# Fewer, larger transfers on one queue: weight copies of three rows, and one store for each output block

## The chip, the core and the metric

The kernel runs on one core of a Trainium2 chip. The metric is the time of one execution on the device in microseconds (us), and the median over runs is compared. TensorE is called PE below, VectorE DVE, ScalarE ACT, GpSimd POOL and SyncE SP, as in the profile. SP computes nothing: its instructions issue DMA transfers, in order, on one hardware queue.

## The reference

Attention with a sigmoid in place of the softmax, followed by a token-mixing layer that makes its mixing weights from its own input. All inputs and the output are float32.

```python
# q, k, v: (8, 12, 448, 64)
scores = q @ k^T / sqrt(64) - log(448)          # per batch and head
attn   = sigmoid(scores) @ v
x      = attn, heads side by side               # (8, 448, 768)
wq, wk = x @ w_q, x @ w_k                       # w_q, w_k: (768, 64)
W      = wq wk^T / sqrt(64)                     # (448, 448) per batch, token to token
mixed  = W @ x                                  # computed as wq @ (wk^T @ x)
out    = relu(mixed) @ w_out                    # w_out: (768, 768)
```

## The kernel before

**Units of work.** The 12 heads of a batch are taken in groups of four, a *quad*; there are 8 x 3 = 24 of them. For a quad, q, k and v are loaded (each 448.0 KB of float32 on 128 partitions), cast to bfloat16 mostly by POOL, arranged and transposed, and then seven score tiles are formed by PE (L319), put through the sigmoid by ACT (L324), and multiplied with v by PE (L341). The 448 tokens are dealt out as 64 partitions of 7 tokens each. When the three quads of a batch are done, the token-mixing layer follows for that batch.

**The order of work** is a string of letters written out by hand, `PLAN`, which is walked once while the program is built: `S` a score tile, `P` a values tile, `C` a copy of output weights, `O` (and `o`, `Q`, `I`, `i`) a part of the output product, and so on. Each engine executes what falls to it in that order and waits on semaphores for what it needs. Where a letter issues a DMA, it goes to SP at that place. The loads have an order of their own, `ORDER`; a load is issued as soon as one of the eight load buffers is free, which is when the load eight places before it has been cast. SP waits for that buffer in its queue, and what was put behind the load waits too.

**The output weights** lie in `wout16`, an array of 128 partitions x 12 rows x 768 columns in bfloat16. Rows 0 to 5 are w_out as loaded, by two transfers of POOL. Rows 6 to 11 are the second arrangement: the same six rows with the two halves of the partitions exchanged. It is made by DMA copies inside the on-chip memory (L864), two for each letter `C`, one row each. Only the batches 2 to 5 use it: their output products (`out_pair`, L530) work on quarters of the PE array, take a half of the contraction from each half of the partitions, and step through the row numbers given by `slot`; twelve steps in four groups of three, of which the last two groups use rows 9 to 11 of the arrangement.

**The output** of a pair of batches `w` is formed in blocks. For the pairs 0 and 3 a block `m` is 128 rows: two tokens per partition group, `y` = 0 in partitions 0 to 63 and `y` = 1 in partitions 64 to 127, with 768 columns. The product (L611) is formed in two halves of 384 columns, each copied from PSUM into the array `o` by ACT or DVE (L644), and then `store` (L621) sends the array out: one transfer for each `y`, 64 partitions x 768 columns. Token `i` of batch `b` goes to rows `i`, `7 + i`, `14 + i`, ... of that batch's output. Block `m` = 3 of a pair has its first half in one batch and its second in the next. Some blocks are formed by another function (`out_halves`, L570, stores at L584), and the pairs 1 and 2 by `out_pair` (copied at L541 or L543, stored at L551). All three take `o` from one pool of three arrays, so the fourth block after another writes into the array from which that one was stored, once that store has landed.

After the last score tile the kernel is in its *tail*: `store` then uses SP for one half and ACT's queue for the other. The last block of all is stored in pieces of 384 columns or fewer.

Of the kernel before, what the change touches and what calls it, by code (L numbers as in the profile page):

```python
# [17 lines left out]
def kernel(  # L18
# [12 lines left out]
    nc = tc.nc  # L31
    B, H, S, HD = q.shape
    D = H * HD
# [3 lines left out]
    NI, NP = 7, 64  # L37
    NU = B
    NJ = H // 4
    NC = D // P  # L40
    NB = D // 2
    HALF = (slice(0, 64), slice(64, 128))
# [45 lines left out]
    def bank2():  # L88
        lo, hi = (int(b) for b in BANKS.pop())
        take(lo, hi)  # L90
        assert hi == lo + 1
        return (lo, hi), banks[:, lo : hi + 1], banks16[:, lo : hi + 1]

    def bank1():
        b = int(BANKS.pop())
        take(b)
        return (b,), banks[:, b], banks16[:, b]

    def read(fb, inst, keep=False):

        for b in fb:
            for old in readers[b][0]:
                if not keep and old.ins.engine != inst.ins.engine:
                    tc.declare_no_dep(inst.ins, old.ins, reason="both only read the bank")
            readers[b][1].append(inst)

    wout16 = singles.tile([P, 2 * NC, D], BF16, name="wout16")
# [406 lines left out]
    def slot(half, b):  # L514

        return b // 2 + (0 if b % 2 == half else NC)

    def out_pair(act, split):

        if opened:  # L520
            w, blocks, part, fb, ps = opened.pop()
        else:
            w, blocks = chunks.pop(0)
            part = 0
            fb, ps, _ = bank2()
        mx = mxs[w].rearrange("p (u b x) -> p u b x", u=2, b=12)
        for b in range(3 * part, 3 * part + 3):
            for y, (u, i) in enumerate(blocks):
                for x in range(2):
                    nc.tensor.matmul(  # L530
                        ps[HALF[x], y, 0:NB], mx[HALF[y], u, b, 64 * (i - 3 * y) : 64 * (i - 3 * y) + 64],
                        wout16[HALF[y], slot(y, b), x * NB : (x + 1) * NB],
                        start=(b == 0), stop=(b == 11),
                    )
        if part < 3:
            opened.append((w, blocks, part + 1, fb, ps))
            return
        o = p_o.tile([P, 2, NB], F32, tag="o", name="o")
        if split:
            for y in range(2):  # L540
                read(fb, COPY["vs"[y]](out=o[:, y], in_=ps[:, y, 0:NB]), keep=True)  # L541
        else:
            read(fb, COPY["s" if act else "v"](out=o, in_=ps[:, :, 0:NB]), keep=True)  # L543
        (u0, i0), (u1, i1) = blocks
        for x in range(2):
            cols = slice(x * NB, (x + 1) * NB)
            if u0 == u1:
                dst = out[2 * w + u0].rearrange("(p i) d -> p i d", i=NI)[:, i0 : i1 + 1 : i1 - i0, cols]
            else:
                dst = out[2 * w : 2 * w + 2].rearrange("b (p i) d -> i p b d", i=NI)[i0, :, :, cols]  # L550
            nc.sync.dma_start(out=dst, in_=o[HALF[x]])  # L551
# [41 lines left out]
    def out_chunk(act, tail):  # L593

        if opened:
            w, m, nb, fb, ps = opened.pop()
            part = 1
        else:
            w, m, nb = chunks.pop(0)
            if nb < 0:  # L600
                nb = 0
                chunks.insert(0, (w, m, 1))
            fb, ps, _ = bank1()
            part = 0
        if nb == 0 and not part:
            ot[0] = p_o.tile([P, D], F32, tag="o", name="o")
        o = ot[0]

        def block(ps, w0, w1, c0, c1):
            for c in range(c0, c1):  # L610
                nc.tensor.matmul(  # L611
                    ps, mxs[w][:, 2 * S * c + m * P : 2 * S * c + (m + 1) * P],
                    wout16[:, c, w0:w1], start=(c == 0), stop=(c == NC - 1),
                )

        last = w == NU // 2 - 1 and m == NI - 1

        def store(cols, eng=nc.scalar if tail else nc.sync):
            for y in range(2):
                b, i = divmod(2 * m + y, NI)  # L620
                (eng if y else nc.sync).dma_start(  # L621
                    out=out[2 * w + b].rearrange("(p i) d -> p i d", i=NI)[:, i, cols],
                    in_=o[HALF[y], cols],
                )

        if nb and last:

            if part:
                fb, ps, _ = bank1()
            h = NB // 2  # L630
            c0 = NB + part * h
            block(ps[:, 0:h], c0, c0 + h, 0, NC)
            read(fb, nc.vector.tensor_copy(out=o[:, c0 : c0 + h], in_=ps[:, 0:h]), keep=True)
            if part:
                store(slice(NB, D))
            else:
                opened.append((w, m, nb, fb, ps))
            return
        ps = ps[:, 0:NB] if not part else ps
        block(ps, nb * NB, (nb + 1) * NB, part * NC // 2, (part + 1) * NC // 2)  # L640
        if not part:
            opened.append((w, m, nb, fb, ps))
            return
        read(fb, COPY["s" if act or last else "v"](out=o[:, nb * NB : (nb + 1) * NB], in_=ps), keep=True)  # L644
        if last:
            store(slice(0, NB))
        elif nb:
            store(slice(0, D))
# [24 lines left out]
    def cols(r):  # L673
# [9 lines left out]
        out=ident, in_=ident, compare_op=ALU.not_equal, fill=1.0, base=0,  # L683
# [135 lines left out]
    for t in PLAN:  # L819
        if t == "F":  # L820
            nc.tensor.matmul(bank1()[1], zeros[:, 0:P], zeros, start=True, stop=True)
            continue
        if t in "12":
            cast_next("vs"[int(t) - 1])
            continue
        kind = ALIKE.get(t, t if t in "qkx" else t.upper())
        c = done[kind]
        done[kind] += 1
        tail = done["S"] == N * NI
        if t == "S":  # L830
            scores(*divmod(c, NI))
        elif kind == "P":
            n, i = divmod(c, NI)
            values(n, i, tail or t == "R", "s" if t == "p" else "v")
            if i == NI - 1:
                used.add(("v", n))
                pump()
        elif kind in "qk":
            if t in "rs":
                quads_r.append(c) if t == "r" else None  # L840
                if t == "s":
                    quadrants(c, 0)
            tr(c, kind, t)
            if t in "df":
                used.add(("q", c))
            if t not in "cers":
                used.add((kind, c))
                pump()
        elif t == "g":
            move()  # L850
        elif t == "z":
            n = quads_r.pop(0)
            quadrants(n, 1)
            used.update({("q", n), ("k", n)})
            pump()
        elif t == "K":
            tr_part("k", k016, KB, "v")
        elif kind == "x":
            tr_x(c, tail, t in "XY", "s" if t in "yY" else "v")
        elif kind == "W":  # L860
            mlp_wqk(*divmod(c, NC), tail, t in "wl", t in "Ll")
        elif kind == "C":
            for y in range(2):
                nc.sync.dma_start(out=wout16[HALF[y], NC + c, :], in_=wout16[HALF[1 - y], c, :])  # L864
        elif kind == "N":
            mlp_wkn(c)
        elif kind == "U":
            (mlp_tmp_tiled if t in "Tt" else mlp_tmp)(c, t in "ut")
        elif kind == "M":
            u, x = divmod(c, NC // 2)  # L870
            mlp_mix(u, x, t == "m", tail or t == "G")
            if x == NC // 2 - 1:
                if u // 2 in TW:
                    chunks.extend((u // 2, ((u % 2, i), (u % 2, 6 - i))) for i in range(3))
                    if u % 2:
                        chunks.append((u // 2, ((0, 3), (1, 3))))
                else:
                    chunks.extend((u // 2, m, -1) for m in (range(3, NI) if u % 2 else range(3)))
        elif kind == "O":
            if (opened or chunks)[0][0] in TW:  # L880
                out_pair(t == "o", t == "Q")
            elif t in "Ii":
                out_halves(t == "i")
            else:
                out_chunk(t in "oQ", tail)
            if not opened:
                allowed[0] = 2
                pump_loads()
                pump()
# [29 lines left out]
```

## Time and profile before

| | |
|---|---|
| median of 3 runs | 182.45 us |
| all three | 180.83, 182.45, 184.24 us |
| profiled execution, first to last instruction (its span) | 180.4 us |
| instructions | 7849 |
| moved by DMA | 47.29 MB, 262 GB/s over the span |
| mean granted TensorE clock | 1.000 |

The three runs are times of whole executions. Of the profiled one the profile gives the span, which is 0.4 us below the fastest run and 2.0 below the median. In the profile, L with a number is a line of the kernel; a tile is named as output `<-` inputs. A digit in a row of slices is the busy share in tenths, and a slice is a fortieth of the span, 4.5 us. Rows of DMA issues give the size of one transfer in KB of 1,024 bytes and the median time from its issue to its landing. In a row with `|`, the time before it is busy time, and behind it stands the idle time before those instructions, with what ended it.

### The profile page before, as it was taken

How to read it: one execution, taken by the hardware profiler on the slowest of the kernel's cores; microseconds unless marked ns; L12 is line 12 of the kernel's file. 1: busy time of each engine (PE TensorE's matmuls, PEld its weight loads, DVE VectorE, ACT ScalarE, POOL GpSimd, SP SyncE). 2: the span in 40 equal slices, each digit the busy share in tenths (PEclk: the TensorE clock that was granted, in tenths of full speed). 3: DMA queues.
4: the chain of work that ended last, by engine and by line, in shares of the span. 5: the costliest groups of instructions: out<-in, count | busy, mean ns of one | idle time of the engine just before them, and what ended most of it. 6: DMA issues, size and time to landing. Idle time of an engine off the chain costs nothing.

```text
span 180.4 us, 7849 instructions
## 1 busy us (share of the span) xinstructions
PE 170.3 (94%) x3412; PEld 114.1 (63%) x3412; DVE 143.7 (80%) x226; ACT 159.0 (88%) x208; POOL 122.9 (68%) x167
## 2 busy tenths in 40 slices
PE   7898899889999999999999999999999999999990
PEld 7444445444675555546667786677888888888660
DVE  3566899998988896989999999978789885868351
ACT  4599999999999999999999999998999989976310
POOL 1076899798999999999999999889978810010000
PEclk9999999999999999999999999999999999999999
DMA  5999999999999989699997999968596432505876
GB/s 169 353 394 346 325 385 376 283 304 366 339 305 358 349 266 299 226 318 349 279 318 277 257 307 329 372 215 272 137 336 166 131 88 48 137 4 123 207 196 174
DMA packets 24914, 47.29 MB, mean 262 GB/s; under 512 B 3888, under 2 KB 18480, under 8 KB 24880
## 3 DMA queue, kind: packets, MB, share of 16 engines
q1 hardware_dynamic: 23600, 44.64, 76.8%
q0 software_dynamic: 800, 1.18, 3.6%
q10 hardware_dynamic: 480, 0.98, 1.5%
q8 instruction: 26, 0.43, 0.9%
q14 instruction: 8, 0.07, 0.1%
HBM read 35.78 MB, written 11.01 MB: 259 GB/s over the span
## 4 chain that ended last, share of the span: by engine, by line
PE 61%; DMA 16%; ACT 7%; POOL 5%; DVE 4%; SPq 3%; issue 2%; POOLq 0%
PE banks L530 15%; PE banks L341 11%; PE banks L319 11%; PE banks L611 9%; DMA k<-in_k_dram 8%; ACT at L324 7%; DMA v<-in_v_dram 5%; DMA w<-in_moe_w_k_dram 4%; PE banks L570 3%; POOL qk L192 2%; PE banks L404 2%; PE banks L416 2%; PE banks L379 2%; PE banks L363 2%; PE banks L484 1%
## 5 line engine op out<-in xcount | busy, mean ns | idle before, releaser
L324 ACT ACTIVATE at<-banks 128x896 bf16<-128x896 f32 x168 | 139.8, 951 | 2.9 <-PE banks L319 2.4
L319 PE MATMUL banks<-qk 64*64 64x448 bf16 x672 | 62.0, 357 | 3.3 <-ACT at L324 2.0
L341 PE MATMUL banks<-at,v 64*64 64x448 bf16 x672 | 47.3, 351 | 0.8 <-ACT at L324 0.7
L319 PEld LDWEIGHTS <-qk 64*64 64x64 bf16 x672 | 25.7, 105 | 21.5 <-issue 13.3
L530 PE MATMUL banks<-wout,mx 64*64 64x384 bf16 x672 | 36.2, 323 | 0.0
L192 POOL CAST qk<-k 128x896 bf16<-128x896 f32 x19 | 22.7, 1196 | 10.1 <-DMA k<-in_k_dram 9.7
L341 PEld LDWEIGHTS <-v 64*64 64x64 bf16 x672 | 23.2, 106 | 8.4 <-issue 1.8
L350 DVE CAST xt<-banks 128x896 bf16<-128x896 f32 x22 | 23.8, 1084 | 2.5 <-PE banks L341 2.0
L530 PEld LDWEIGHTS <-mx 64*64 64x64 bf16 x672 | 22.6, 107 | 4.5 <-issue 0.2
L611 PE MATMUL banks<-wout,mx 128*128 128x384 bf16 (+1 forms) x138 | 24.4, 320 | 0.0
L192 POOL CAST qk<-q 128x896 bf16<-128x896 f32 x18 | 21.5, 1193 | 2.5 <-DVE qk L276 1.0
L471 DVE TENSOR_SCALAR mx<-banks 128x1024 bf16<-128x1024 f32 (+3 forms) x22 | 21.3, 970 | 1.9 <-PE banks L484 0.7
L209 POOL CAST v<-v 128x896 bf16<-128x896 f32 x22 | 20.6, 952 | 1.8 <-DMA v<-in_v_dram 1.3
L611 PEld LDWEIGHTS <-mx 128*128 128x128 bf16 x138 | 12.3, 98 | 9.8 <-issue 3.2
L167 POOL COPY qk<-swap 32x448 uint32<-32x448 uint32 x28 | 16.3, 584 | 1.6
L276 DVE STREAM_TRANSPOSE qk<-qk 128x448 f32<-128x448 f32 x28 | 17.0, 628 | 0.5 <-POOL qk L164 0.4
L161 POOL COPY swap<-qk 32x448 uint32<-32x448 uint32 x28 | 15.6, 556 | 2.5 <-DVE qk L192 0.8
L164 POOL COPY qk<-qk 32x448 uint32<-32x448 uint32 x28 | 15.6, 555 | 1.6
L245 DVE STREAM_TRANSPOSE qk<-qk 32x448 f32<-32x448 f32 x24 | 15.3, 636 | 0.6
L413 POOL COPY wq<-wqk 64x448 bf16<-64x448 bf16 x3 | 1.7, 556 | 15.8 <-DVE wqk L412 15.8
L644 DVE COPY o<-banks 128x384 f32<-128x384 f32 x12 | 6.6, 553 | 5.7 <-PE banks L611 5.3
L392 DVE COPY xn<-banks 128x1024 bf16<-128x1024 bf16 (+1 forms) x14 | 8.8, 625 | 2.8 <-PE banks L379 2.7
(89 smaller groups left out, 203.8 us busy)
## 6 DMA issues: line engine op xcount, KB each, us to landing
q<-in_q_dram SPq DMA_DIRECT2D x24, 448.0 KB, 6.3
v<-in_v_dram SPq DMA_DIRECT2D x24, 448.0 KB, 6.0
k<-in_k_dram SPq DMA_DIRECT2D x23, 448.0 KB, 6.9
out_dram<-o SPq DMA_DIRECT2D x50, 192.0 KB, 4.2
wout<-in_moe_w_out_dram POOLq DMA_DIRECT2D x2, 576.0 KB, 11.6
wout<-wout SPq DMA_DIRECT2D x12, 96.0 KB, 6.4
out_dram<-o ACTq DMA_DIRECT2D x4, 192.0 KB, 3.2
k<-in_k_dram SPq DMA_DIRECT2D x1, 256.0 KB, 4.8
```

The costliest lines, as they stand in the source:

```text
L161: eng.tensor_copy(out=z[lo], in_=w[hi, 0])
L167: eng.tensor_copy(out=w[lo, 1], in_=z[lo])
L192: COPY[e](out=f[:, :, "qk".index(nm)].rearrange("p e i d y -> p e y i d"), in_=ld.pop((nm, n)).rearrange("p (y i e d) -> p e y i d", y=2, ...
L209: COPY[e](out=t16.rearrange("p b i d -> p (b i d)"), in_=ld.pop((nm, n)).rearrange("p b x -> p (b x)"),)
L276: nc.vector.transpose(out=qk[n][:, t].rearrange("p t i n -> p (t i n)").bitcast(F32), in_=w)
L319: nc.tensor.matmul(sc[HALF[h], g, 0:S], qk[n][HALF[g], h, 1, i, :], qk[n][HALF[g], h, 0].rearrange("p i n -> p (i n)"), start=True, stop=True,
L324: inst = nc.scalar.activation(at, sc[:, :, 0:S], ACTF.Sigmoid, bias=attn_bias, scale=attn_scale)
L341: nc.tensor.matmul(ps[HALF[g], h, 0:S], ld["v16", n][HALF[h], g, i, :], ats[n, i][HALF[h], g, :], start=(i == 0), stop=(i == NI - 1),)
L350: read(fb, COPY[eng](out=xt(u, j)[:, :, 0:S], in_=ps[:, :, 0:S]))
L471: inst = nc.vector.tensor_scalar(dst, ps, moe_scale, 0.0, ALU.mult, ALU.max)
L530: nc.tensor.matmul(ps[HALF[x], y, 0:NB], mx[HALF[y], u, b, 64 * (i - 3 * y) : 64 * (i - 3 * y) + 64], wout16[HALF[y], slot(y, b), x * NB : ...
L611: nc.tensor.matmul(ps, mxs[w][:, 2 * S * c + m * P : 2 * S * c + (m + 1) * P], wout16[:, c, w0:w1], start=(c == 0), stop=(c == NC - 1),)
```

## The change

Two edits, both in what SP issues.

1. For the letter `C`, instead of two copies of one row at each of six places, one copy of three rows at four of them. Places 0 and 3 fill the first half of the partitions, places 1 and 4 the second; places 2 and 5 issue nothing.
2. Outside the tail, and where all 768 columns of a block are stored, `store` issues one transfer from the whole array `o`, 128 partitions. The destination is an access pattern written by hand, whose outermost dimension has two entries (the two tokens, `step` apart), the next 64 (steps of seven rows), and the last 768 columns.

```diff
+    def rows(b0, i0, b1, i1):
+
+        step = (b1 - b0) * S * D + (i1 - i0) * D
+        assert step > 0
+        return out[b0].rearrange("(p i) d -> p i d", i=NI)[:, i0], [step, 2]
...
         def store(cols, eng=nc.scalar if tail else nc.sync):
+            if not tail and cols == slice(0, D):
+                (b0, i0), (b1, i1) = divmod(2 * m, NI), divmod(2 * m + 1, NI)
+                at, lead = rows(2 * w + b0, i0, 2 * w + b1, i1)
+                nc.sync.dma_start(out=bass.AP(at.tensor, at.offset, [lead, [NI * D, NP], [1, D]]), in_=o)
+                return
             for y in range(2):
                 b, i = divmod(2 * m + y, NI)
                 (eng if y else nc.sync).dma_start(
...
         elif kind == "C":
-            for y in range(2):
-                nc.sync.dma_start(out=wout16[HALF[y], NC + c, :], in_=wout16[HALF[1 - y], c, :])
+            if c % 3 < 2:
+                y, lo = c % 3, c // 3 * 3
+                nc.sync.dma_start(
+                    out=wout16[HALF[y], NC + lo : NC + lo + 3, :], in_=wout16[HALF[1 - y], lo : lo + 3, :],
+                )
```

## The prediction

> **What bounds the kernel now.** I read the page first, for the span, the engines' shares and the transfers' level over time; then the chain in order of time, to see where transfers set the pace and where they don't; then the views of the SP queue, because both edits live there.
>
> ```profile
> span 180.4 us, 7849 instructions
> PE 170.3 (94%) x3412; PEld 114.1 (63%) x3412; DVE 143.7 (80%) x226; ACT 159.0 (88%) x208; POOL 122.9 (68%) x167
> DMA  5999999999999989699997999968596432505876
> GB/s 169 353 394 346 325 385 376 283 304 366 339 305 358 349 266 299 226 318 349 279 318 277 257 307 329 372 215 272 137 336 166 131 88 48 137 4 123 207 196 174
> q1 hardware_dynamic: 23600, 44.64, 76.8%
> ```
>
> The 16 DMA engines are 90% busy or close to it until about slice 26 (117 us), and nearly everything goes through one queue, q1, which is SP's. So whatever one store adds to an engine of that queue stands ahead of the loads issued after it.
>
> ```profile
> 29.29 13.64 DMA k<-in_k_dram
> ...
> 51.54 0.68 PE banks L570 x12
> ...
> 93.29 0.60 PE banks L530 x12
> ...
> 94.30 0.49 PE banks L530 x12
> ...
> 94.97 0.49 PE banks L530 x12
> ...
> 166.29 9.89 PE banks L611 x66
> 176.20 0.36 DVE o L633
> ```
>
> In the chain in order of time the last load stands at 29.29 (it lands at 42.9). From 51.5 on the chain is PE's with a few ACT pieces and no transfer. TensorE is the bound there, and a transfer counts only when it gets late enough to stop PE. PE has no spare time to win that back.
>
> Two speeds of a DMA engine are needed. The fastest slice moved 394 GB/s over 16 engines: 24.6 kB per us each. The q1 row gives the slow end: 44.64 MB in 76.8% of 16 x 180.4 us is 20.1 kB per us of busy time, waits for memory included.
>
> **The copies of the output weights.** Twelve transfers of 96 KB become four of three rows (288 KB): the bytes are the same.
>
> ```profile
> L864 SPq DMA_DIRECT2D wout<-wout x12: 467/522/897, 41.7 to 87.8; - x12
> SPq L173 <- POOL qk L192: 12.9, 7, 3.3
> SPq L179 <- POOL v L209: 8.1, 3, 4.2
> wout<-wout SPq DMA_DIRECT2D x12, 96.0 KB, 6.4
> ```
>
> Eight issues fall away, 8 x 0.52 = 4.2 us of SP. I count them as nothing: the load lines L173 and L179 wait longest for POOL to free a buffer, so SP has time, and nothing of SP stands in the chain at these times. The bounds are 0 and a gain of 4.2. In the plan the four copies go out where copies 0, 1, 3 and 4 stood (41.66, 46.49, 78.82, 85.25); copies 2 and 5 have none of their own. Row 3 of the second half, until now sent at 78.8, moves back to 85.25. It is first read in the third group of the first output pair, at 94.97. Issued at 85.25 it would land 6.4 later, at 91.7: still 3.3 early, so this edit alone costs nothing. That cover is thin, though, and the other edit takes it away.
>
> **The stores, what leaves.** Six blocks of the first two batches go out at 52.66, 67.78, 76.17, 81.84, 90.19 and 98.63, each as two transfers of 64 rows, 192.0 KB. Each becomes one of 384 KB. Six issues fall away.
>
> ```profile
> L621 SPq DMA_DIRECT2D out_dram<-o x18: 466/494/771, 52.7 to 176.6; - x18
> ```
>
> That is 6 x 0.49 = 2.9 us of SP, again beside POOL's waits: taken as 0, bounds 0 and a gain of 2.9. The tail's stores are halves of 384 columns or go out by SP and ACT as before, so the end after 169 us is untouched.
>
> **The stores, what arrives.** The source is the whole array: 128 partitions of 3,072 bytes. The destination is now written as 2 x 64 x 768, with the count of 2 outermost. No other transfer of this kernel has that: in the code every load has 128 rows outermost on both sides, every copy and store 64. No row shows what a DMA does with an outermost count of 2. If the work is dealt out over the engines along the outermost dimension, 64 and 128 can be dealt to 16 engines and 2 to only two.
>
> So there are two ends. At the wide end (all 16 engines) the store has the bytes of the two it replaces and costs nothing more. At the narrow end half the store, 196,608 bytes, goes through one engine: 196,608 / 24.6 kB = 8.0 us, against 24,576 bytes or 1.0 us on each engine now. I take the narrow end. The rows nearest to it by size, the stores of 64 rows, differ from it in just the count by which work can be dealt out, so they don't speak for the wide end.
>
> The Trainium skill says, on the page "DMA: Bandwidth & Descriptors", section "Why a DMA increments its semaphore by 16 and not by 1", that the number of engines is the largest up to 16 that divides the slowest dimension larger than 1 of both sides. By that rule the new store runs on 2 engines and everything now in the trace on 16; no run here shows the former, and the 394 GB/s agree with the latter.
>
> **How late things get at the narrow end.** Work on one engine's part of q1 is done in the order of issue:
>
> ```profile
> DMA to landing us min/median/max: 2.7/4.0/7.3
> ```
>
> This is for L551's stores: 2.7 when little is ahead, 7.3 in the busy stretch, and the 96 KB copies above took 6.4 for half the bytes. Waiting behind others is most of it. All later loads use all engines, so each needs the two loaded ones. Now the queue behind the first of these stores, by issues. The first fence is the SP queue, the second the issues from 53.9 to 85.2, the third those from 88.75 to 98.6.
>
> ```profile
> 51.10 1.43 SPq L173 DMA_DIRECT2D k<-in_k_dram  x2
> 52.66 1.18 SPq L621 DMA_DIRECT2D out_dram<-o  x2
> ...
> 85.25 3.45 SPq L864 DMA_DIRECT2D wout<-wout  x4
> ...
> 98.63 1.11 SPq L621 DMA_DIRECT2D out_dram<-o  x2
> ```
>
> ```profile
> v<-in_v_dram SPq DMA_DIRECT2D x6, 448.0 KB, 5.4
> q<-in_q_dram SPq DMA_DIRECT2D x6, 448.0 KB, 5.8
> k<-in_k_dram SPq DMA_DIRECT2D x4, 448.0 KB, 6.4
> out_dram<-o SPq DMA_DIRECT2D x8, 192.0 KB, 5.1
> ```
>
> ```profile
> v<-in_v_dram SPq DMA_DIRECT2D x3, 448.0 KB, 6.0
> q<-in_q_dram SPq DMA_DIRECT2D x2, 448.0 KB, 5.1
> k<-in_k_dram SPq DMA_DIRECT2D x1, 448.0 KB, 3.8
> ```
>
> The second k load ahead of the first store goes out near 51.6 and lands some 6.9 us later (the page's median for k), at 58.5. Up to the copy of 85.25 the engine then has four stores (32.0), 16 loads of 28,672 bytes each (1.17, together 18.7), one block stored in halves (1.0) and the copies of 78.82 and 85.25 (18,432 bytes, 0.75 each). 58.5 + 32.0 + 18.7 + 1.0 + 1.5 = 111.7. The matmuls that need this copy stood at 94.97: **PE stops 16.7 us.**
>
> Then come 6 loads (7.0) and stores five and six (16.0): the sixth lands at 134.7. There are three output arrays, so the third block after the sixth store waits for it before it can be copied out of PSUM:
>
> ```profile
> 96.25 0.80 ACT L543 COPY o<-banks 128x768 f32<-128x768 f32 x1 [0.19 <-PE banks L530]
> ...
> 107.69 0.96 DVE L543 COPY o<-banks 128x768 f32<-128x768 f32 x1
> 108.59 0.69 DVE L471 TENSOR_SCALAR mx<-banks 128x512 bf16<-128x512 f32 x1
> 109.36 1.09 DVE L350 CAST xt<-banks 128x896 bf16<-128x896 f32 x1
> ```
>
> The blocks after the sixth store are copied at 96.25, 104.98 and 107.69; the last of them waits until 134.7, **27.0 us late**. VectorE works in order, so the ReLU at 108.59 and the cast at 109.36, for which PE waits, queue behind it. The two delays overlap: 16.7 is had in any case, and 10.3 more as far as PE can't run on without VectorE. I take the middle, 21.8. The loads behind the sixth store land from 135.9 on, 1.2 us apart; the quads that use them are shifted by the same waits, so I count nothing more for them.
>
> **The sum.** 180.4 + 0 (copies) + 0 (issues) + 21.8 = 202.2 of span. The runs shown have a median of 182.45, 2.0 over that span, so the predicted time is 204.2, rounded to **204**.
>
> **The rivals.** First, not slower: **the store is dealt to all 16 engines.** Then the bytes per engine are as before, SP has up to 7.1 us less to issue, and no wait of the chain ends there: 182.5, at best some 2 less. For it speaks that the present transfers all reach the full rate; against it only the count of 2. The Trainium skill, same page, section "Rules for kernel authors", advises one transfer of 128 partitions instead of two of disjoint halves, because both halves use the same 16 engines; by that advice alone the edit is harmless or good. It decides if the store's landing stays near 5 us. Chance 8%.
>
> Second: **two engines, but another pair each time.** Then the pairs work side by side and a load is held up by one store at most. The copy of 85.25 would land at 91.7 + 7.0 = 98.7, 3.7 late: 184.1 of span, 186.2. For it: nothing in the rows fixes which engines are taken. Against it: the loads need every engine, so any pair delays them. Chance 4%.
>
> Third: **the narrow end at the slow speed of 20.1 kB per us.** A store takes 9.8, a load 1.43: the copy lands at 58.5 + 39.1 + 22.9 + 3.0 = 123.5 (28.5 late) and the sixth store at 123.5 + 8.6 + 19.6 = 151.7 (44.0 late); the middle is 36.2, the time 218.7. For it: it is the mean of the whole run. Against it: with 14 engines starved there is less to wait for. Chance 6%.
>
> **How the numbers follow.** The forecast has 82%. The range is 190 to 220: it holds the forecast with its own bounds (199 with only the first wait, 209.4 with the whole second one), a shorter queue than I count, and the third rival; it leaves out the first two, 12%, and some tails. A measurement of this kernel can tell about 2% from no change, 3.6 us. Faster by more: 3%, from the first rival. Within: 7%, the rest of the first and half of the second. Slower: 90%.
>
> **What would show it.** Right: six issues of 384 KB landing after 13 us or more instead of 5; GB/s well down between 60 and 135 us while loads still wait; PE idle in front of L530 near 95 until a wout transfer lands; ACT or DVE idle before L543 or L644 until a store lands. Four copies of 288 KB, the last landing past 105. Wrong: landings of 5 to 7 us for the 384 KB stores, which would be the first rival; stores of 10 us without PE idle at 95, the second; an idle PE elsewhere first (at the scores, for want of k or q) would mean that the loads and not the copy decide.

## The result, and the profile after

The changed kernel takes **207.46 us** (median of 4 runs, 206.65 to 209.88), against 181.64 for the kernel before in the same comparison: a ratio of 1.138 (95% interval 1.128 to 1.149). It is slower by some 25 us, on the side and near the time that was forecast. Ratios, here and below, leave out runs that fell in a slower state, so they differ a little from the quotients of the medians. The profiled execution took 206.91 us, with a span of 205.1, so 24.7 more than before.

The page of the changed kernel, with PEclk added because it is no longer full speed throughout:

```profile
span 205.1 us, 7831 instructions
PE 177.7 (87%) x3412; PEld 119.2 (58%) x3412; DVE 144.1 (70%) x226; ACT 160.0 (78%) x208; POOL 122.4 (60%) x167
PE   8888898899899699992946994299999999999991
PEclk9999999999999999998596999669999999999999
DMA  6999999999998677491818449597569643423685
GB/s 181 368 379 335 378 388 283 304 386 278 236 383 324 210 232 270 149 300 74 255 55 261 159 147 301 162 312 241 165 221 290 212 124 80 95 65 83 165 218 156
PE 42%; DMA 36%; POOL 11%; DVE 4%; SPq 2%; issue 1%; ACT 1%; POOLq 0%; DVEq 0%; ACTq 0%
```

A slice is 5.1 us now. From the thirteenth on the 16 DMA engines are busy 10 to 80% in many slices instead of 90%, and GB/s falls as low as 55, while the loads are late. How few of the 16 still have work there is shown below, in the row for 103 to 107 us. PE has six slices at 2 to 6 tenths in that stretch. Transfers hold 36% of the chain that ended last (16% before).

The issues, with the median time to landing in the last column:

```profile
q<-in_q_dram SPq DMA_DIRECT2D x24, 448.0 KB, 11.1
v<-in_v_dram SPq DMA_DIRECT2D x24, 448.0 KB, 11.5
k<-in_k_dram SPq DMA_DIRECT2D x23, 448.0 KB, 9.7
out_dram<-o SPq DMA_DIRECT2D x6, 384.0 KB
wout<-wout SPq DMA_DIRECT2D x4, 288.0 KB, 12.8
```

The six stores and four copies are there. The loads land after 10 to 11.5 us (medians) instead of 6 or 7. The profile gives no landing for the new stores; the records of their single packets in the trace end 13 to 18.5 us after each store's issue.

The chain in order of time has the two forecast waits, one after the other, and an earlier one that was not forecast:

```profile
54.77 13.34 DMA q<-in_q_dram
...
90.23 19.25 DMA wout<-wout
...
112.71 18.25 DMA out_dram<-o
...
131.15 0.97 DVE o L549
```

The copy lands at 90.23 + 19.25 = 109.5 (forecast 111.7), and the output product behind it, now L536, goes on. The sixth store lands at 112.71 + 18.25 = 131.0 (forecast 134.7). Only then does VectorE copy the block that stood at 107.69 before: at 131.15, 23.5 us later. The groups of waits say the same from the side of the engines:

```profile
DVE o L549 <- DMA out_dram<-o: 7.3, 1, 7.3
PE banks L319 <- DVE o L549: 6.9, 1, 6.9
PE banks L536 <- DMA wout<-wout: 4.7, 1, 4.7
ACT o L655 <- DMA out_dram<-o: 4.7, 1, 4.7
POOL qk L192 <- DMA k<-in_k_dram: 18.5, 4, 9.1
```

PE's wait for the copy is 4.7 us, not 16.7, because it came to that place late already, at 104.8 instead of 94.97: VectorE had waited 2.1 us for the load that begins at 54.77, ACT 4.7 us for a store before it could copy into `o`, and the granted clock had fallen (last section).

### The profile page after: what moved, and what is told of

Its sections match the earlier page's. It is cut to its first block, busy times and chain, and to the rows that moved or that the text cites. A ratio compares the mean times of both kernels' runs of the same rounds, so it can differ in the third digit from the quotient of the medians.

```text
span 205.1 us, 7831 instructions
## 1 busy us (share of the span) xinstructions
PE 177.7 (87%) x3412; PEld 119.2 (58%) x3412; DVE 144.1 (70%) x226; ACT 160.0 (78%) x208; POOL 122.4 (60%) x167
## 4 chain that ended last, share of the span: by engine, by line
PE 42%; DMA 36%; POOL 11%; DVE 4%; SPq 2%; issue 1%; ACT 1%; POOLq 0%; DVEq 0%; ACTq 0%
DMA q<-in_q_dram 12%; PE banks L536 12%; DMA wout<-wout 9%; DMA out_dram<-o 9%; PE banks L341 7%; PE banks L617 7%; PE banks L319 7%; POOL qk L192 5%; DMA k<-in_k_dram 3%; DMA w<-in_moe_w_k_dram 3%; PE banks L576 2%; PE banks L404 2%; PE banks L379 1%; POOL v L209 1%; PE banks L460 1%
## 5 line engine op out<-in xcount | busy, mean ns | idle before, releaser
L319 PE MATMUL banks<-qk 64*64 64x448 bf16 x672 | 64.6, 369 | 11.5 <-DVE o L549 6.9
L341 PE MATMUL banks<-at,v 64*64 64x448 bf16 x672 | 51.0, 372 | 0.7 <-ACT at L324 0.7
L319 PEld LDWEIGHTS <-qk 64*64 64x64 bf16 x672 | 26.4, 108 | 30.8 <-issue 22.5
L536 PE MATMUL banks<-wout,mx 64*64 64x384 bf16 x672 | 38.2, 332 | 4.7 <-DMA wout<-wout 4.7
L192 POOL CAST qk<-k 128x896 bf16<-128x896 f32 x19 | 22.6, 1193 | 22.5 <-DMA k<-in_k_dram 18.5
L341 PEld LDWEIGHTS <-v 64*64 64x64 bf16 x672 | 26.5, 113 | 8.3 <-issue 1.8
L536 PEld LDWEIGHTS <-mx 64*64 64x64 bf16 x672 | 23.9, 110 | 9.5 <-issue 5.1
L192 POOL CAST qk<-q 128x896 bf16<-128x896 f32 x18 | 21.5, 1192 | 12.2 <-DVE qk L276 7.9
L617 PE MATMUL banks<-wout,mx 128*128 128x384 bf16 (+1 forms) x138 | 24.4, 320 | 0.1
L167 POOL COPY qk<-swap 32x448 uint32<-32x448 uint32 x28 | 15.5, 552 | 1.6
L655 ACT COPY o<-banks 128x384 f32<-128x384 f32 x9 | 4.4, 490 | 12.2 <-PE banks L617 6.4
L549 DVE COPY o<-banks 128x768 f32<-128x768 f32 x8 | 7.6, 954 | 8.5 <-DMA out_dram<-o 7.3
## 6 DMA issues: line engine op xcount, KB each, us to landing
v<-in_v_dram SPq DMA_DIRECT2D x24, 448.0 KB, 11.5
```

Of the source, the lines that this page charges most:

```text
L192: COPY[e](out=f[:, :, "qk".index(nm)].rearrange("p e i d y -> p e y i d"), in_=ld.pop((nm, n)).rearrange("p (y i e d) -> p e y i d", y=2, ...
L319: nc.tensor.matmul(sc[HALF[h], g, 0:S], qk[n][HALF[g], h, 1, i, :], qk[n][HALF[g], h, 0].rearrange("p i n -> p (i n)"), start=True, stop=True,
L341: nc.tensor.matmul(ps[HALF[g], h, 0:S], ld["v16", n][HALF[h], g, i, :], ats[n, i][HALF[h], g, :], start=(i == 0), stop=(i == NI - 1),)
L536: nc.tensor.matmul(ps[HALF[x], y, 0:NB], mx[HALF[y], u, b, 64 * (i - 3 * y) : 64 * (i - 3 * y) + 64], wout16[HALF[y], slot(y, b), x * NB : ...
L617: nc.tensor.matmul(ps, mxs[w][:, 2 * S * c + m * P : 2 * S * c + (m + 1) * P], wout16[:, c, w0:w1], start=(c == 0), stop=(c == NC - 1),)
```

## The experiments

Ratios are to the kernel before, run beside each kernel; the medians of the latter were 182.5 to 183.6 us.

| | median, us | ratio | 95% interval |
|---|---|---|---|
| e1, copies alone | 182.54 | 1.000 | 0.995 to 1.006 |
| e2, stores alone | 206.22 | 1.129 | 1.118 to 1.141 |
| e3, 128 outermost | 183.06 | 1.000 | 0.995 to 1.005 |
| e4, 62 and 2 rows | 207.73 | 1.136 | 1.126 to 1.146 |
| e5, 60 and 4 rows | 182.89 | 1.002 | 0.997 to 1.007 |
| e6, copies early | 206.67 | 1.135 | 1.124 to 1.146 |
| e7, seven output arrays | 204.25 | 1.123 | 1.112 to 1.135 |
| e8, both | 203.30 | 1.116 | 1.106 to 1.126 |
| e9, first three stores | 191.53 | 1.053 | 1.043 to 1.062 |
| e10, 57 and 7 rows | 193.39 | 1.061 | 1.048 to 1.073 |
| e11, stores by ACT | 210.68 | 1.157 | 1.143 to 1.170 |
| e12, 128 outermost by ACT | 188.58 | 1.038 | 1.030 to 1.046 |

**Which edit, and which property of it (e1 to e3).** The first is the kernel before with the new copies, the second the changed kernel with the old ones. The third keeps both edits and changes the destination's shape, which sends the rows of these six blocks to other places of the output:

```diff
-                (b0, i0), (b1, i1) = divmod(2 * m, NI), divmod(2 * m + 1, NI)
-                at, lead = rows(2 * w + b0, i0, 2 * w + b1, i1)
-                nc.sync.dma_start(out=bass.AP(at.tensor, at.offset, [lead, [NI * D, NP], [1, D]]), in_=o)
+                both = out[2 * w : 2 * w + 2].rearrange("b s d -> (b s) d")
+                nc.sync.dma_start(out=both.rearrange("(p i) d -> p i d", i=NI)[:, m], in_=o)
```

> The copies alone are changed (four of three rows), the stores stay two transfers of 64 rows. Two engines (my theory): the stores alone make the time, so this is 180 to 184 us, as before, and the last copy lands before 95 us. Copies (rival: the larger copies, and row 3 of the second half sent later, stop PE): 195 us or more, with PE waiting in front of the output pairs for a wout transfer. Size (rival: any large transfer holds up the queue): 288 KB instead of 96 KB, so 183 to 188.

> The stores alone are changed, the copies stay twelve of one row. Two engines: 203 to 210 us, nearly all of the loss, because the last copies of one row stand behind the fourth store just as the copies of three rows do. Copies: back near 182. Size: 200 or more, as two engines.

> As the changed kernel, the same six single stores of 384 KB from 128 partitions, but the destination counts 128 rows (seven rows apart) outermost, not 2 x 64. The rows of these six blocks so go to other tokens of the output than the reference has; bytes, rows of 3,072 bytes and all other work are as in the changed kernel. Two engines: the store is dealt to 16 engines, lands in about 4 to 8 us, and the time is 180 to 184. Size: one transfer of 384 KB still holds up the queue, 200 or more. Copies: 200 or more, since the copies are the changed ones.

The copies cost nothing and bring nothing; the stores alone make the loss; and a store of the same size, from the same 128 partitions, in rows of the same 3,072 bytes, makes none when the destination counts 128 outermost. The rivals "copies" and "size" fall. The stores and the span of e3:

```profile
span 182.2 us, 7830 instructions
out_dram<-o SPq DMA_DIRECT2D x6, 384.0 KB, 8.1
```

They land after 8.1 us (median), in the queue's busiest stretch.

**How the engines are chosen (e4, e5, e10).** A count of 2 could be special, or it could be one case of a divisor. These three take the kernel before and cut each store of 64 rows outside the tail in two; `n` is 62, 60 or 57:

```diff
+                dst = out[2 * w + b].rearrange("(p i) d -> p i d", i=NI)[:, i, cols]
+                if not tail:
+                    for r in (slice(0, n), slice(n, NP)):
+                        nc.sync.dma_start(out=dst[r], in_=o[64 * y + r.start : 64 * y + r.stop, cols])
+                    continue
```

> The kernel before, with each store of 64 rows outside the tail issued as 62 rows and 2 rows, on SP; no count of 2 is added in front of the 62. Dealt by a divisor (62 = 2 x 31, so two engines, and two for the 2 rows): each block puts the same bytes on two engines as the changed kernel, 201 to 212 us, with PE stopped in front of the output pairs and copies of o waiting for stores. Dealt in turn over up to 16 engines (rival: only a small outermost count narrows a transfer): 62 rows go to all 16, 181 to 185, the 12 more issues of 0.5 us beside POOL's waits.

> As the run with 62 and 2 rows, but 60 and 4 rows: the same number of issues, two rows moved from one to the other. Dealt by the largest divisor up to 16: 60 rows on 15 engines and 4 rows on 4, at most 4 x 3,072 more bytes on any engine than before: 181 to 186 us. If splitting a store and its extra issues were what costs: 200 or more, as with 62 and 2.

> The kernel before with each store outside the tail as 57 and 7 rows. Dealt by the largest divisor up to 16, 57 = 3 x 19 goes to three engines: 19 rows for each of two stores, 116,736 bytes a block, about 4.3 us, 3.6 more than before with the 7 rows; six blocks add 22 us, of which 13 are taken up: 189 to 195. Dealt over all engines: 181 to 186.

All three came out as the divisor has it. Two rows moved from one transfer to the other are worth 25 us, with the same issues, bytes and destination.

The trace shows the engines themselves. This is the changed kernel from 103 to 107 us, while its fourth narrow store is under way; the last two numbers are the DMA share and GB/s:

```profile
103.00:107.00 4.00, 1.84 (x46) 1.09 (x39) 2.18 (x3) 2.54 (x3) 2.86 (x4) 1.00 0.13 52
```

A share of 0.13 is two of 16 engines, with 26 GB/s each; the other 14 have nothing to do. The trace also has a record of every packet, and a row of 3,072 bytes is one packet. On one engine they follow each other at 0.118 us. The packets of these stores start at some 17 per us with 2 x 64 and with 62 rows, which is two engines' worth, and at some 26 per us with 57 rows, three engines' worth; with 128, 64 and 60 rows 17 to 19 of them are at times under way at once, all 16 engines' worth, since packets on one engine overlap a little. (Whether the profile gives a store's landing is no sign: with 62 and 57 rows it gives none for the loads either.)

The Trainium skill's rule (page "DMA: Bandwidth & Descriptors", section "Why a DMA increments its semaphore by 16 and not by 1") is the largest divisor up to 16: 2 for 62, 3 for 57, 15 for 60. The times agree with it in all five shapes tried: 2 x 64, 128, 62, 60, 57. The packets show the 2 and the 3; 15 is not told apart from 16. The advice of the Trainium skill (same page, section "Rules for kernel authors"), one transfer of 128 partitions instead of two halves, proved harmless in e3 and bought nothing (1.000); with a count of 2 in front of the destination the one transfer is 13.8% slower.

**Which wait decides (e6 to e8).** The prediction named two: PE for the copy and VectorE for a free output array. The first edit takes away the one, the second the other, and e8 has both:

```diff
-            if c % 3 < 2:
-                y, lo = c % 3, c // 3 * 3
-                nc.sync.dma_start(
-                    out=wout16[HALF[y], NC + lo : NC + lo + 3, :], in_=wout16[HALF[1 - y], lo : lo + 3, :],
-                )
+            if c == 1:
+                for y, lo in ((0, 0), (1, 0), (0, 3), (1, 3)):
+                    nc.sync.dma_start(
+                        out=wout16[HALF[y], NC + lo : NC + lo + 3, :], in_=wout16[HALF[1 - y], lo : lo + 3, :],
+                    )
```

```diff
-    p_o = pool("o", 3)
+    p_o = pool("o", 7)
```

> The changed kernel with all four copies of output weights issued at the second place of the plan (about 45 us), before the first store. Theory with two waits in a row: PE no longer waits for a wout transfer in front of the output pairs, but ACT's and DVE's copies into o still wait for stores, until about 131 us: 201 to 207, so at most 6 us come back. Rival (the copy's wait is the one that decides): 190 to 195.

> The changed kernel with seven output arrays instead of three, copies where the change has them. Two waits: no copy into o waits for a store any more; PE still waits for the wout transfer until about 109 us and goes on from there: 194 to 201. Rival (the output arrays alone decide): 184 to 190. Rival (late loads decide): 204 to 208, as changed.

> Both: copies early and seven output arrays, with the narrow stores kept. What is left is the lateness of the loads behind the stores on the two engines. If the prediction was right to count nothing for it: 183 to 187. If the loads alone are late enough to stop PE: from the queue (six stores of 8 us and 28 loads of 1.17 us behind 58.5 us) the k of quad 20 lands near 141 us, and its scores began at 131: 190 to 200, with POOL waiting for k and q and PE's scores for the transposes.

e6 is inside its expectation. e7 misses its own by 3 us and lies in the range of the rival that late loads decide. e8 is the surprise: with both waits gone 203.3 us are left, more than even the rival allowed. Its chain has loads where the changed kernel has the copy and the store:

```profile
57.40 13.13 DMA q<-in_q_dram
...
71.71 14.04 DMA k<-in_k_dram
...
113.79 18.75 DMA k<-in_k_dram
```

```profile
ACT at L324 <- PE banks L319: 23.6, 19, 6.8
POOL qk L192 <- DMA k<-in_k_dram: 20.7, 5, 8.9
...
POOL qk L192 <- DMA q<-in_q_dram: 8.0, 3, 6.3
```

The k load issued at 113.79 lands at 132.5, right behind the sixth store, and POOL, then PE, then ACT run dry. So the copy, the free output array and the loads are three readers of one late queue, and each alone is late by nearly the whole amount. Taking the wait from one hands it to the next. What decides is the work on the two engines, not who reads it.

**How much work, and in whose queue (e9, e11, e12).** e9 is the changed kernel with one more condition:

```diff
-            if not tail and cols == slice(0, D):
+            if not tail and cols == slice(0, D) and m < 4:
```

> The changed kernel with only the first three blocks stored by the narrow transfer, the other three by two of 64 rows. Theory (the queue of the two engines, with slack before anything stops): six narrow stores add 6 x 6.3 = 38 us to that queue (7.2 instead of 0.9 each) and cost 24.7, so some 13 us are taken up by the loads' lead. Three add 19, of which 13 are taken up: 186 to 191. Rival (each narrow store costs its own share): half of the loss, 194 to 197. Rival (the loss comes from the last stores, next to the output pairs): 182 to 185.

191.5 us, half a microsecond above the theory's range and well below the 194 to 197 of equal shares. Three stores cost 9 us, the next three 16. By the packet times, a narrow store is 64 rows or 7.5 us for each of the two engines, where 8 rows or 0.9 us were. This gives estimates: of the three stores' 20 us of added work 11 were taken up, of the six stores' 40, 15, and of e10's 23, 12. So the first 11 us or so of lateness look hidden by the lead of the loads, and most of the rest shows.

In e11 and e12 `nc.sync` becomes `nc.scalar` in the store of the changed kernel and of e3.

> The changed kernel with the narrow store issued by ACT instead of SP, so it stands in another queue of the same engines. Theory one, order within SP's queue: loads and copies no longer stand behind a store, the two engines alternate, and a load is slowed to at most twice its 1.2 us while a store runs: 183 to 190. Theory two, the bytes on the two engines: the same 38 us more work for them, 198 to 207. ACT may also wait at the issue for DVE's half of a block, up to 1 us a block.

> The run with 128 rows outermost (tokens of these six blocks misplaced, as there), its six stores issued by ACT instead of SP: the price of ACT's issuing by itself. All theories: 182 to 187.

Both miss. e12 is 1.6 us above its expectation: issuing by ACT costs some 5.5 us by itself (nearer 7 by the ratios), in an ACT that is 88% busy in the kernel before. e11 is 3.7 us above the range of theory two, which left that price out. Over e12, e11 is 22.1 us slower (210.68 - 188.58); on SP the narrow store cost 24.4 over the wide one (207.46 - 183.06). Taking the stores out of the loads' queue so brought 2 or 3 us of some 25: theory two. By its packets the first narrow store takes 13.9 us in e11 instead of 8.1, since the two engines also carry the loads meanwhile. The order within SP's queue was the way I worked the sum, and it is not what makes the loss. The same two engines must carry the bytes, from either of the two queues.

**No version beats the kernel before.** e1, e3 and e5 are equal to it within 0.7%. A single wide store with its tokens in the right place needs the two tokens interleaved over the partitions, which the layout of `mx` doesn't give to the matmul; it wasn't tried, and e3 says that there is nothing to win by it.

## Why the prediction was right, and where not

- **The direction, and the narrow end: right, and shown.** The changed kernel against e3 isolates the outermost count; e4, e5 and e10 show that the count works through its divisors, and the packets show two and three engines.
- **The copies at nothing: right** (e1: 1.000), and so were the issues saved: e3 has 14 fewer and is no faster.
- **A store of 8.0 us: a little too long.** By its packets one engine's 64 rows take 7.5 us, 26 kB per us; the fastest slice of all 16 engines (24.6) was no upper bound for two. From its first packet to its last a store takes 7.9 to 8.1 us, because the two engines don't begin and end together. Between the copy's landing (109.5) and the sixth store's (131.0) the two engines carried what SP issued in between:

```profile
97.10 0.78 SPq L173 DMA_DIRECT2D k<-in_k_dram  x1
97.97 1.14 SPq L173 DMA_DIRECT2D q<-in_q_dram  x1
99.22 0.88 SPq L628 DMA_DIRECT2D out_dram<-o  x1
100.19 7.55 SPq L173 DMA_DIRECT2D q<-in_q_dram  x1
107.84 4.78 SPq L179 DMA_DIRECT2D v<-in_v_dram  x3
112.71 0.52 SPq L628 DMA_DIRECT2D out_dram<-o  x1
```

  Two stores at 7.5 leave 6.4 of these 21.5 us for six loads, 1.1 each where I had 1.17. With the copy 2.2 us earlier than forecast, that moved the sixth store from 134.7 to 131.0.
- **The first wait of 16.7 "in any case": wrong as a wait of PE.** PE came to it 9.9 us late, from earlier waits and a slower clock that I had not counted, and waited 4.7; without this wait (e6) the kernel is less than 1 us faster.
- **The half of the second wait: wrong.** I let PE run on for half of the 10.3 us in which VectorE alone would wait. VectorE's copy came 23.5 us late and the end 24.7 late, so on balance PE won none of it back. The full term with the measured landing gives 23.5 where I had 21.8: a sixth store that was put too late and a wait that was halved partly cancel, and that 204 came so near 207.5 is in part luck.
- **Nothing more for the loads: right as a sum, wrong as a reason.** They added nothing to the two waits, but e8 shows that they would have cost 20 us without them. I had named the first two readers of the late queue as the cause.
- **"Work is done in the order of issue" within q1: not needed.** e11 has the stores in another queue and loses nearly as much.
- **The third rival (20.1 kB per us) and the second (another pair each time) fall:** the former by the 7.5 us, the latter because the fifth store, issued at 99.22, sends its first packet at 110.45, after the fourth's last at 107.95; other pairs would have worked side by side.
- **Signs:** the six stores that end 13 us or more after their issue (by their packets), the fall in GB/s, L549 and L655 waiting for stores, PE waiting for wout, and the last copy's landing past 105 all came. But PE first stood idle elsewhere, for 1.6 us at 69.9, behind VectorE's wait for the load issued at 54.77: the sign that I had given for the loads being late enough to decide.

## What to carry to other kernels

Before merging two transfers, look at the outermost dimension of both sides that the merged one will have, and at its largest divisor up to 16: in the five shapes tried here that, not the bytes or the partitions, says how many engines carry it, and 62 rows are as bad as 2. A narrow transfer delays every wide one that shares its engines, from SP's queue and from ACT's, and the harm shows up at whichever engine reads late data first, so undoing the waits one by one gives back little (1 to 4 of 25 us here); compare GB/s with the loads' time to landing instead. Where transfers already hide behind POOL's and PE's work, fewer issues on SP buy no time.

## What the runs showed that was not expected

**The granted clock fell.** It was 1.00 in every stretch of the kernel before. These are the stretches 50 to 110 and 110 to 140 us of the changed kernel; behind each engine's busy time come the clock, the DMA share and GB/s:

```profile
50.00:110.00 60.00, 49.04 (x780) 28.82 (x776) 40.50 (x59) 46.17 (x59) 50.50 (x70) 0.94 0.70 227
110.00:140.00 30.00, 23.07 (x414) 16.87 (x409) 17.31 (x25) 18.62 (x23) 11.25 (x15) 0.84 0.70 230
```

PE's busy time grew by 7.4 us (170.3 to 177.7) for the same 3412 matmuls. The trace's records of the clock have only full and half speed, and half speed three times within the kernel: from 95.7 to 102.5, 109.4 to 112.8 and 129.9 to 136.7 us. PE waited longer than 1.6 us just three times, for 3.3, 4.7 and 6.9 us, and these waits end at 95.9, 109.5 and 132.2. The stalls so cost twice, once as idle time and once as slower work behind them; how much of the 7.4 lies on the path to the end was not separated. The Trainium skill (page "TensorE: Matmul & The Clock Gate", Part 1) has the clock halved after some 3.4 us of idleness and back after as long a busy stretch. The trace agrees with the halving and with its following idle stretches; three waits are too few to show the threshold.

**SP was held up while issuing.** A q load issued at 100.19, right behind a narrow store, took 7.55 us to issue (the row is above); in the kernel before single loads took 0.33 to 1.8. What SP issues behind it waits too, and while that load was being issued the row for 103 to 107 us has 14 engines idle. Each of the four transfers right behind the third to the sixth narrow store took 6.6 to 7.6 us to issue. In e10 no load took more than 2.0 us and some 11 us were lost, and in e11 none more than 3.1 with a loss as large, so this is a companion of the loss and not its cause.
